# Three more chunks of 512 tokens with seven products, and two batch transforms packed closer

## The chip, the core and the metric

The kernel runs as one program on one core of a Trainium2 chip. TensorE (PE) multiplies matrices: a weight load (PEld) puts up to 128x128 numbers into the array and a matmul streams columns past them into PSUM. VectorE (DVE), ScalarE (ACT) and GpSimd (POOL) work on vectors, and the queues of SyncE (SP), ACT and POOL issue DMAs. Each engine takes its instructions in the written order. The metric is the device time of one execution in microseconds (us); lower is better.

## The reference

A real Fourier transform over the 3008 tokens of each of four batches, a complex 256x256 mixing with bias and soft threshold, the inverse transform, and then a feed-forward layer with a leaky rectifier over all 12032 tokens:

```python
X = np.fft.rfft(x, axis=1)                       # x: (4, 3008, 256)
Yr = Xr @ w_r - Xi @ w_i + b_r
Yi = Xr @ w_i + Xi @ w_r + b_i
Yr = np.sign(Yr) * np.maximum(np.abs(Yr) - 0.01, 0.0)   # Yi likewise
y = np.fft.irfft(Y, n=3008, axis=1)
h = y @ w_in                                     # (12032, 256) x (256, 2048)
g = np.maximum(h, 0.0) + alpha * np.minimum(h, 0.0)
out = g @ w_out                                  # (2048, 256)
```

## The kernel before

**Numbers in two parts.** Most operands are split into a high and a low part (`hi` by ACT, `lo = x - hi` by DVE or POOL), and a product is three matmuls: hi by hi, hi by the weights' low part, lo by hi.

**The transform of a batch** has four parts, for each of which the program has short functions. *Row parts* (`a_load`, `a_split`, `a_mm`, `a_evac`; 16 groups g per batch) go through DRAM (`ad`); *column parts* (`b_load`, `b_mm`, `b_evac`, the mixing `m_*`, `c_mm`, `c_evac`; 12 pairs q per batch) read `ad` and write `zd`. The last part (`d_load`, `d_mm`, `d_part`) reads 376 tokens of `zd`, transforms them by 16 small matmuls (L611) and splits them into `yh`, `yl`, the input of the feed-forward layer. All use the three PSUM buffers `ps_f`.

**The feed-forward layer in two forms.** The first `CC` = 24 chunks (mostly 384 tokens) go through 16 steps each: `l1_step` does six matmuls of 384 columns (L672), ACT and DVE make `q` (L678, L679) and split it (L683, L684), and `l2_step`, three steps later, does nine matmuls of 256 columns (L709 to L711). From token 8960 on six chunks of 512 tokens follow, each as eight pairs of steps (`s_l1`, `s_l2`). A pair has twelve matmuls of 512 columns (L775); then, instead of eight products of 256 columns (24 matmuls, the pairs named in `PLAIN`, and all of the last chunk), six pairs of the eight use Strassen's scheme: sums of blocks (L790 to L810) and seven products (21 matmuls, L871 to L873). It needs sums of blocks of the weights, made once by `w_full`, `w_sums`, `w_split` near the end of the main steps, in the space of the transform's tables. After a chunk's eighth pair `s_out` (L890) joins the products in PSUM by three copies on ACT and eight additions on DVE; only then are the two `ps_o` buffers free for the next chunk's products. `s_turn` transposes and stores. Chunks and their matmuls run two pairs (`SLAG`) apart.

**What sets the order.** The main steps are numbered 0 to NS - 1 (NS = 384). A table `todo` says behind which step another piece of work is written; `mid` does so for the middle of a step, `pre` and `post` for the pairs. In the main steps the batches' transforms stand at fixed distances: row groups every 2 steps, column pairs every 6, batch 2 from step 137 (rows) and 172 (columns), batch 3 from 241 and 276. The column parts of batch 2 and the row parts of batch 3 share only a few steps (239 to 246), and step 256 begins a chunk of 256 tokens. At the very start `keep_warm(WARM)` puts 40 small matmuls (L964) on PE between the row parts and the first column product of batch 0 (`b_mm`, L426).

```python
WARM = 40
o = s0 + 44 - (SHIFT if b == 2 else 0); i = o + 6 * q     # column pair q of batch b + 1
```

Of the kernel before, what the change touches and what calls it, by code (L numbers as in the profile page):

```python
# [93 lines left out]
def fft_mix_moe(ctx, tc, x, w_r, w_i, b_r, b_i, w_in, w_out, alpha, la, rb, lc, rd, lf, cf, sel, out):  # L94
# [12 lines left out]
    TC = 384  # L107
    assert NC * TC - 128 == NC * TOK

    CC = 24  # L110
    SC = 512

    def head(c):
# [9 lines left out]

    const = ctx.enter_context(tc.tile_pool(name="const", bufs=1))
    work = ctx.enter_context(tc.tile_pool(name="work", bufs=2))
    dram = ctx.enter_context(tc.tile_pool(name="dram", bufs=2, space=bass.MemoryType.DRAM))
    ps_f = ctx.enter_context(tc.tile_pool(name="ps_f", bufs=3, space=bass.MemoryType.PSUM))
    ps_h = ctx.enter_context(tc.tile_pool(name="ps_h", bufs=2, space=bass.MemoryType.PSUM))
    ps_o = ctx.enter_context(tc.tile_pool(name="ps_o", bufs=2, space=bass.MemoryType.PSUM))
# [503 lines left out]
        ds[dg] = [d_mm(t, ct) for ct in range(CT)]  # L633

    def s_dpart(dg, n):
        for k, n0, n1, a, z in s_parts(dg):
            if k == n:
                for ct in range(CT):
                    if n == NS2 - 1:
                        d_part(ds[dg][ct], ct, n0, n1, *(y[:, :, a:z] for y in yt[CC + n]))  # L640
                    else:
                        s_dput(ds[dg][ct][:, :, n0:n1], [y[:, ct] for y in yt[CC + n]], a // CH, z // CH)

    def s_dput(ps, ys, u, u1):

        ys = [y.rearrange("p (g i j) -> p g i j", i=CH, j=32) for y in ys]
        n = 0
        while u < u1:
            if u % 32 == 0 and u1 - u >= 32:
                w = (u1 - u) // 32 * 32  # L650
                src = ps[:, :, n:n + w].rearrange("p i (g j) -> p g i j", j=32)
                dst = [y[:, u // 32:(u + w) // 32] for y in ys]
            else:
                w = min(u1, u // 32 * 32 + 32) - u
                src = ps[:, :, n:n + w]
                dst = [y[:, u // 32, :, u % 32:u % 32 + w] for y in ys]
            split(src, *dst, A, V)
            u += w
            n += w

# [73 lines left out]
        for k in range(4):  # L734
            sw[k] = a[:, k], (a[:, 4 + k] if k < 2 else b[:, k - 2])

    wf = []

    def w_full(p):

        h, m = divmod(4 * p, FH)
        w = wo_h[h][:, m:m + 4]
        t = work.tile([128, 4, C], F32, tag="xt", name="wo_f")
        V.tensor_tensor(out=t, in0=f(w[:, :, 0]), in1=f(w[:, :, 1]), op=ALU.add)
        s = work.tile([128, 4, 2, 128], F32, tag="xt", name="wo_s")
        wf.extend((t.rearrange("p (r j) (c h) -> p j h r c", j=2, h=2), s))

    def w_sums(p, k):

        t, s = wf  # L750
        x, y, op = ((t[:, 0, 1], t[:, 1, 1], ALU.add), (s[:, 0], t[:, 0, 0], ALU.subtract),
                    (t[:, 0, 0], t[:, 0, 1], ALU.subtract), (t[:, 1, 0], s[:, 1], ALU.subtract))[k]
        V.tensor_tensor(out=s[:, k], in0=x, in1=y, op=op)

    def w_split(p):
        _, s = wf
        wf.clear()
        a, b = (t[:, :, 2 * p:2 * p + 2] for t in sw["all"])
        A.activation(out=a[:, 0:4], in_=s, func=AF.Copy)
        V.tensor_tensor(out=a[:, 4:6], in0=s[:, 0:2], in1=f(a[:, 0:2]), op=ALU.subtract)  # L760
        V.tensor_tensor(out=b, in0=s[:, 2:4], in1=f(a[:, 2:4]), op=ALU.subtract)


    sg, sa = {}, {}
# [125 lines left out]
    def s_out(n):  # L890
        a, b, c = sa.pop(n)
        e = [work.tile([128, HS], F32, tag="q", name="se", bufs=3) for _ in range(3)]
        u = [work.tile([128, HS], F32, tag="gh", name="su", bufs=4) for _ in range(3)]
        c1 = work.tile([128, 2, HS], F32, tag="Yt", name="c1", bufs=1)
        c2 = work.tile([128, 2, HS], F32, tag="Yc", name="c2", bufs=1)
        A.activation(out=e[0], in_=a[:, 0], func=AF.Copy)
        A.activation(out=e[1], in_=c[:, 1], func=AF.Copy)
        A.activation(out=e[2], in_=o_last[:, 1], func=AF.Copy)
        V.tensor_tensor(out=c1[:, 1], in0=a[:, 1], in1=e[0], op=ALU.add)
        V.tensor_tensor(out=u[0], in0=c[:, 0], in1=e[0], op=ALU.add)  # L900
        V.tensor_tensor(out=u[1], in0=e[2], in1=e[1], op=ALU.subtract)
# [64 lines left out]
    with tc.manual_schedule():  # L966
# [111 lines left out]
        for b in range(B):  # L1078
            s0 = b * per
            for g in range(J if b == 0 else 0, min(NCH, CC - NCH * b)):  # L1080
                i = s0 + g * FT
                at(i - 8, d_load, b, g)
                at(i - 4 if i == J * FT else i - FT + 1, d_open, NCH * b + g)
                if b == 0 and g == J:
                    at(i - DS, d_step, b, g)
                else:
                    at(i - 3, d_step, b, g)
            if b + 1 < B:
                o = s0 + 4 - (SHIFT if b == 2 else 0)
                for g in range(NG):  # L1090
                    if b == 0 and g >= FILL:
                        i = 6 * (g - FILL) + 9
                        if g % 2 == 0:
                            at(i - 8, a_load, 1, g // 2)
                        at(i, a_mm, 1, g)
                        at(i, a_evac, 1, g)
                    if b == 0:
                        continue
                    if g % 2 == 0:
                        at(o + 2 * g - 2, a_load, b + 1, g // 2)  # L1100
                    at(o + 2 * g + 3, a_split, b + 1, g)
                    at(o + 2 * g + 5, a_mm, b + 1, g)
                    at(o + 2 * g + 5, a_evac, b + 1, g)
                o = s0 + 44 - (SHIFT if b == 2 else 0)
                for q in range(NPAIR):
                    i = o + 6 * q
                    if b == 0:
                        i = PB + 11 * q // 2
                    at(i - BL, b_load, b + 1, q)
                    at(i, b_mm, b + 1, q)  # L1110
                    at(i, b_evac, b + 1, q)
                    at(i, b_evac2, b + 1, q)
                    at(i + MM, m_mm, b + 1, q)
                    at(i + M2, m_mm2, b + 1, q, when=mid)
                    for n, k in enumerate(MP):
                        at(i + k, m_part, b + 1, q, n, when=mid)
                    at(i + MP[6], m_evac1, b + 1, q)
                    at(i + CM, c_mm, b + 1, q)
                    at(i + CM, c_evac, b + 1, q)

        spairs = [(n, t) for n in range(NS2) for t in range(PR)]
        pre, post = {}, {}
        i = NS - SHIFT - 4
        at(i, w_open)
        for p in range(PR // 2):
            at(i + 5 * p, w_full, p)
            for k in range(4):
                at(i + 5 * p + 1 + k // 2, w_sums, p, k)
            at(i + 5 * p + 3, w_split, p)
        at(NS - 14, d_open, CC)  # L1130
        for dg in range(CC, B * NCH):
            ns = [n for n, *_ in s_parts(dg)]
# [43 lines left out]
        for k in range(len(spairs) + SLAG):  # L1176
# [9 lines left out]
            if k >= SLAG:  # L1186
# [42 lines left out]
```

## Time and profile before

| what | value |
|---|---|
| median of 3 runs | 1397.45 us (1396.28 to 1398.24) |
| the profiled execution | 1399.11 us, of which the span of instructions is 1397.3 us |
| PE busy | 1375.3 us, 98% |
| DVE, ACT, POOL busy | 873.9 us (63%), 728.1 us (52%), 401.0 us (29%) |
| chain that ended last | PE 86%, DVE 6%, ACT 3%, issue 2%, DMA 1% |

How to read it: matmuls overlap, so a matmul's duration (0.28 us for 256 columns) is longer than the distance from its start to the next one's start (about 0.12 us); distances of starts give PE's pace. An idle time in a row is the pause of the engine ahead of it, with what ended it. Main steps run until 1118 us, the chunks of 512 from there to the end.

### The profile page before, as it was taken

How to read it: one execution, taken by the hardware profiler on the slowest of the kernel's cores; microseconds unless marked ns; L12 is line 12 of the kernel's file. 1: busy time of each engine (PE TensorE's matmuls, PEld its weight loads, DVE VectorE, ACT ScalarE, POOL GpSimd, SP SyncE). 2: the span in 40 equal slices, each digit the busy share in tenths (PEclk: the TensorE clock that was granted, in tenths of full speed). 3: DMA queues.
4: the chain of work that ended last, by engine and by line, in shares of the span. 5: the costliest groups of instructions: out<-in, count | busy, mean ns of one | idle time of the engine just before them, and what ended most of it. 6: DMA issues, size and time to landing. Idle time of an engine off the chain costs nothing.

```text
span 1397.3 us, 25329 instructions
## 1 busy us (share of the span) xinstructions
PE 1375.3 (98%) x9670; PEld 1316.4 (94%) x9670; DVE 873.9 (63%) x1589; ACT 728.1 (52%) x1518; POOL 401.0 (29%) x454
## 2 busy tenths in 40 slices
PE   8999999999999999999999999999999999999998
PEld 4979899999999999999999999999999998898997
DVE  2666855666564544666665556666656577778874
ACT  3466555545455665454456654445454555555553
POOL 3854832322322222222222223232222211111121
PEclk9999999999999999999999999999999999999999
DMA  9864222101111231111122321111100110111001
GB/s 235 226 191 148 78 91 71 53 25 61 62 47 37 79 85 56 61 53 37 41 76 86 110 65 35 43 61 54 46 20 20 34 35 6 34 27 28 5 12 31
DMA packets 72451, 89.67 MB, mean 64 GB/s; under 512 B 22043, under 2 KB 54782, under 8 KB 72329
## 3 DMA queue, kind: packets, MB, share of 16 engines
q1 hardware_dynamic: 63743, 76.74, 18.8%
q0 software_dynamic: 5168, 8.02, 2.1%
q10 hardware_dynamic: 3418, 3.29, 0.7%
q8 instruction: 76, 1.25, 0.4%
q14 instruction: 46, 0.38, 0.1%
HBM read 50.49 MB, written 34.34 MB: 61 GB/s over the span
## 4 chain that ended last, share of the span: by engine, by line
PE 86%; DVE 6%; ACT 3%; issue 2%; DMA 1%; SPq 0%; ACTq 0%; POOL 0%; DVEq 0%
PE ps_h L672 25%; PE ps_h L775 8%; PE ps_o L710 6%; PE ps_o L711 6%; PE ps_o L709 6%; PE ps_m L486 6%; PE ps_d L611 3%; PE ps_b L426 3%; PE o_last L711 3%; PE o_last L709 3%; PE o_last L710 3%; PE ps_m L473 3%; PE ps_o L871 1%; PE ps_o L872 1%; PE ps_o L873 1%
## 5 line engine op out<-in xcount | busy, mean ns | idle before, releaser
L672 PE MATMUL ps_h<-yh,w 128*128 128x384 f32 (+1 forms) x1472 | 431.2, 335 | 3.7 <-DVE q L679 3.6
L679 DVE SCALAR_TENSOR_TENSOR q<-q,beta_s,ps_h 128x384 f32<-128x384 f32 (+1 forms) x384 | 230.7, 601 | 229.8 <-ACT q L678 227.8
L684 POOL TENSOR_TENSOR gl<-q,gh 128x384 fp32r<-128x384 f32 (+1 forms) x187 | 193.8, 1036 | 597.0 <-ACT gh L683 534.5
L683 ACT ACTIVATE gh<-q 128x384 fp32r<-128x384 f32 (+1 forms) x384 | 198.3, 516 | 274.4 <-DVE q L679 271.0
L672 PEld LDWEIGHTS ps_h<-yh,w 128*128 128x128 f32 x1472 | 271.0, 189 | 7.3 <-DVE q L679 3.8
L678 ACT ACTIVATE q<-ps_h 128x384 f32<-128x384 f32 (+1 forms) x384 | 182.7, 476 | 118.0 <-PE ps_h L672 103.4
L672 PE MATMUL ps_h<-yl,w 128*128 128x384 f32 (+1 forms) x736 | 243.4, 331 | 0.0
L711 PE MATMUL ps_o<-w,gl 128*128 128x256 f32 x768 | 216.1, 281 | 3.0 <-POOL gl L684 3.0
L710 PE MATMUL ps_o<-w,gh 128*128 128x256 f32 x768 | 216.8, 282 | 0.0
L709 PE MATMUL ps_o<-w,gh 128*128 128x256 f32 x768 | 216.0, 281 | 0.0
L684 DVE TENSOR_TENSOR gl<-q,gh 128x384 fp32r<-128x384 f32 (+1 forms) x197 | 115.9, 589 | 66.4 <-ACT gh L683 64.6
L711 PEld LDWEIGHTS ps_o<-w,gl 128*128 128x128 f32 x768 | 145.9, 190 | 3.8 <-POOL gl L684 3.6
L710 PEld LDWEIGHTS ps_o<-w,gh 128*128 128x128 f32 x768 | 145.9, 190 | 0.1
L709 PEld LDWEIGHTS ps_o<-w,gh 128*128 128x128 f32 x768 | 144.6, 188 | 0.1
L672 PEld LDWEIGHTS ps_h<-yl,w 128*128 128x128 f32 x736 | 139.3, 189 | 1.4
L775 PE MATMUL ps_h<-yh,w 128*128 128x512 f32 x384 | 128.0, 394 | 1.9 <-DVE sq L779 1.7
L711 PE MATMUL o_last<-w,gl 128*128 128x256 f32 x352 | 100.6, 286 | 0.0
L709 PE MATMUL o_last<-w,gh 128*128 128x256 f32 x352 | 100.2, 285 | 0.0
L710 PE MATMUL o_last<-w,gh 128*128 128x256 f32 x352 | 100.2, 285 | 0.0
L810 POOL TENSOR_TENSOR l<-t,h 128x512 fp32r<-128x512 f32 x30 | 38.9, 1296 | 191.2 <-ACT h L808 173.8
L775 PEld LDWEIGHTS ps_h<-yh,w 128*128 128x128 f32 x384 | 72.1, 188 | 16.8 <-DVE sq L779 2.5
L779 DVE SCALAR_TENSOR_TENSOR sq<-sq,beta_s,ps_h 128x512 f32<-128x512 f32 x96 | 68.2, 742 | 22.0 <-ACT sq L778 21.8
(209 smaller groups left out, 2727.7 us busy)
## 6 DMA issues: line engine op xcount, KB each, us to landing
zt<-zd SPq DMA_DIRECT2D x32, 384.0 KB
ad<-ast SPq DMA_DIRECT2D x48, 192.0 KB
bt<-ad SPq DMA_DIRECT2D x72, 128.0 KB
zd<-zst SPq DMA_DIRECT2D x36, 256.0 KB
xt<-in_x SPq DMA_DIRECT2D x21, 320.0 KB
cw_s<-in_moe_w_in SPq DMA_DIRECT2D x8, 512.0 KB
cw_s<-in_moe_w_out SPq DMA_DIRECT2D x8, 512.0 KB
out<-os SPq DMA_DIRECT2D x26, 128.0 KB
```

The costliest lines, as they stand in the source:

```text
L426: PE.matmul(ps[:, s, ct], t[:, s, 128 * ct:128 * ct + 128], rb_s[:, 2 * q + s], start=True, stop=True)
L486: PE.matmul(p, a[:, k:k + 128], mix[i][:, w, ct], start=(n == 0), stop=(n == 3 * CT - 1))
L672: PE.matmul(ps, wi_h[m // FH][:, w, ct, 128 * (m % FH):128 * (m % FH) + 128], a[:, ct, 0:n], start=(k == 0), stop=(k == 3 * CT - 1))
L678: A.activation(out=q, in_=ps, func=AF.Relu, scale=-1.0)
L679: V.scalar_tensor_tensor(out=q, in0=q, scalar=beta_s[:, m:m + 1], in1=ps, op0=ALU.mult, op1=ALU.add)
L683: A.activation(out=hi, in_=q, func=AF.Copy)
L684: (V if LOS[(2 * m + c) % len(LOS)] and fill or not fill and (m + c) % 2 else G).tensor_tensor(out=lo, in0=q, in1=f(hi), op=ALU.subtract)
L709: PE.matmul(a, hi[:, t], w[:, 0], start=(i, k) in first, stop=False)
L710: PE.matmul(a, hi[:, t], w[:, 1], start=False, stop=False)
L711: PE.matmul(a, lo[:, t], w[:, 0], start=False, stop=(i, k) in last)
L775: PE.matmul(ps, wi_h[m // FH][:, w, ct, 128 * (m % FH):128 * (m % FH) + 128], a[:, ct], start=(k == 0), stop=(k == 3 * CT - 1))
L779: V.scalar_tensor_tensor(out=q[:, j], in0=q[:, j], scalar=beta_s[:, m:m + 1], in1=ps, op0=ALU.mult, op1=ALU.add)
```

## The change

`CC` is 20, so chunks of 512 tokens begin at token 7424: nine instead of six, eight of them with seven products; NS is 320. In the main steps the transforms of batches 2 and 3 stand by new tables (`AO`, `BO`, `BP`): row groups every 1.5 steps from step 120 and 186, column pairs every 5 steps from 154 and 222. The sums of weights come in six instead of five steps per group, and the split of a group is four instructions in three steps. In the chunks of 512 the splits of the last transform's results are written with all high parts ahead of all low parts; a part that lies wholly in one chunk comes at pair 6 instead of 3 of its place; and a pair's sums of blocks (`s_sums`) are written behind the join of the chunk before (`s_out`) instead of ahead of it. `WARM` is 70.

```diff
-    CC = 24
+    CC = 20
-    dram = ctx.enter_context(tc.tile_pool(name="dram", bufs=2, space=bass.MemoryType.DRAM))
+    dram = ctx.enter_context(tc.tile_pool(name="dram", bufs=4, space=bass.MemoryType.DRAM))
     def s_dpart(dg, n):
...
+                        parts.extend(s_dput(ps, ys, a // CH, z // CH))
+        for src, hi, lo in parts:
+            A.activation(out=hi, in_=src, func=AF.Copy)
+        for src, hi, lo in parts:
+            V.tensor_tensor(out=lo, in0=src, in1=f(hi), op=ALU.subtract)
-    def w_split(p):
+    def w_split(p, k, low):
...
+        if not low:
+            A.activation(out=hi, in_=s[:, 2 * k:2 * k + 2], func=AF.Copy)
+        else:
+            V.tensor_tensor(out=b if k else a[:, 4:6], in0=s[:, 2 * k:2 * k + 2], in1=f(hi), op=ALU.subtract)
+        sq[n, t] = q
+
+    def s_sums(n, t):
+        q = sq.pop((n, t))
-        u = [work.tile([128, HS], F32, tag="gh", name="su", bufs=4) for _ in range(3)]
+        u = [work.tile([128, HS], F32, tag="gh", name="su", bufs=4) for _ in range(4)]
-    SHIFT = 24
+    AO = {2: 120, 3: 186}
+    BO = {2: 154, 3: 222}
+    BP = 5
-    WARM = 40
+    WARM = 70
+                    i = AO[b + 1] + 3 * g // 2
+                i = PB + 11 * q // 2 if b == 0 else BO[b + 1] + BP * q
-        i = NS - SHIFT - 4
+        i = NS - 26
-            at(i + 5 * p + 3, w_split, p)
+            for k in range(2):
+                at(i + 6 * p + 3 + k, w_split, p, k, False)
+                at(i + 6 * p + 4 + k, w_split, p, k, True)
             elif dg > CC:
-                first += 3
+                first += 6
                     if t == PR - 1:
                         s_out(n)
-                if t == 1 and n:
-                    s_turn(n - 1)
+            if k < len(spairs):
+                s_sums(*spairs[k])
+            if k >= SLAG and t == 1 and n:
+                s_turn(n - 1)
```

The first place is DVE at the join of the first chunk of 512. Before (`c` and `su` are the results of `s_out`, `dl` and `l` the low parts of a pair's blocks):

```order
L779 SCALAR_TENSOR_TENSOR sq<-sq,beta_s,ps_h 128x512 x2
L794 TENSOR_TENSOR dl<-sq,dh 128x768
L795 TENSOR_TENSOR l_13993<-sq,h_13992 128x256
L899 TENSOR_TENSOR c_14025<-ps_o,se 128x256
L900 TENSOR_TENSOR su<-ps_o,se 128x256
L901 TENSOR_TENSOR su<-se 128x256
L902 TENSOR_TENSOR su<-su,se 128x256
L903 TENSOR_TENSOR su<-ps_o,su 128x256
L904 TENSOR_TENSOR c_14025<-ps_o,su 128x256
```

And DVE at the same join in the changed kernel:

```order
L788 SCALAR_TENSOR_TENSOR sq<-sq,beta_s,ps_h 128x512 x2
L912 TENSOR_TENSOR c_12440<-ps_o,se 128x256
L913 TENSOR_TENSOR su<-ps_o,se 128x256
L914 TENSOR_TENSOR su<-se 128x256
L915 TENSOR_TENSOR su<-su,se 128x256
L916 TENSOR_TENSOR su<-ps_o,su 128x256
L917 TENSOR_TENSOR c_12440<-ps_o,su 128x256
L918 TENSOR_TENSOR c_12441<-o_last,su 128x256
L919 TENSOR_TENSOR c_12441<-su 128x256
L807 TENSOR_TENSOR dl<-sq,dh 128x768
```

The eight additions of the join now stand directly behind the pair's `sq`, and the low parts `dl`, `l` come after them.

The second place is DVE at the second group of weight sums before (`wo_s` are the sums, `sw_a` and `sw_b` their high and low parts, L679 a step's `q`):

```order
L753 TENSOR_TENSOR wo_s<-wo_f 128x256
L753 TENSOR_TENSOR wo_s<-wo_f,wo_s 128x256
L679 SCALAR_TENSOR_TENSOR q<-q,beta_s,ps_h 128x384
L760 TENSOR_TENSOR sw_a<-wo_s,sw_a 128x2x256
L761 TENSOR_TENSOR sw_b<-wo_s,sw_a 128x2x256
L679 SCALAR_TENSOR_TENSOR q<-q,beta_s,ps_h 128x384
```

And DVE at the second group in the changed kernel:

```order
L761 TENSOR_TENSOR wo_s<-wo_f 128x256
L761 TENSOR_TENSOR wo_s<-wo_f,wo_s 128x256
L687 SCALAR_TENSOR_TENSOR q<-q,beta_s,ps_h 128x384
L692 TENSOR_TENSOR gl<-q,gh 128x384
L687 SCALAR_TENSOR_TENSOR q<-q,beta_s,ps_h 128x384
L692 TENSOR_TENSOR gl<-q,gh 128x384
L770 TENSOR_TENSOR sw_a<-wo_s,sw_a 128x2x256
L687 SCALAR_TENSOR_TENSOR q<-q,beta_s,ps_h 128x384
L770 TENSOR_TENSOR sw_b<-wo_s,sw_a 128x2x256
```

The two low parts of the split no longer stand together behind one copy; each has a step's `q` ahead of it.

The third place is ACT in the changed kernel where row parts of batch 3 (`xh`, `ast`) meet column parts of batch 2 (`Yh`, `Xh`, `sm`), which lay in the same steps only from 239 to 246 before:

```order
L404 ACTIVATE ast<-ps_a 96x512
L139 ACTIVATE xh<-xt 94x512
L686 ACTIVATE q<-ps_h 128x384
L691 ACTIVATE gh<-q 128x384
L723 ACTIVATE ot<-o_last 128x256
L514 ACTIVATE Yh<-Yt 128x512
L440 ACTIVATE Xh<-ps_b 128x2x4x64
L455 ACTIVATE sm<-ps_b 128x2x2x64
L139 ACTIVATE xh<-xt 94x512
L686 ACTIVATE q<-ps_h 128x384
L691 ACTIVATE gh<-q 128x384
```

Between one step's `gh` and the next step's `q` ACT now has five other instructions here, of both transforms and of an output.

## Rows read from the trace of the kernel before

**Rows 1.** Stretches: length; busy PE, PEld, DVE, ACT, POOL; granted clock, DMA share, GB/s.

```profile
460.00:545.00 85.00, 85.00 (x578) 82.20 (x577) 40.87 (x72) 52.51 (x108) 18.58 (x21) 1.00 0.30 86
...
900.00:1000.00 100.00, 100.00 (x747) 100.00 (x746) 62.94 (x121) 49.30 (x106) 25.23 (x32) 1.00 0.15 49
...
1158.00:1298.00 140.00, 136.43 (x874) 123.10 (x873) 112.59 (x211) 74.97 (x149) 23.31 (x18) 1.00 0.10 23
```

**Rows 2.** PE in time, main steps: start, duration.

```profile
1048.35 0.34 PE L672 MATMUL ps_h<-yh,w 128*128 128x384 f32 x1
...
1050.47 0.34 PE L672 MATMUL ps_h<-yh,w 128*128 128x384 f32 x1
```

**Rows 3.** PE in time, pairs of the first chunk of 512.

```profile
1134.42 0.39 PE L775 MATMUL ps_h<-yh,w 128*128 128x512 f32 x1
...
1140.05 0.39 PE L775 MATMUL ps_h<-yh,w 128*128 128x512 f32 x1
...
1145.27 0.40 PE L775 MATMUL ps_h<-yh,w 128*128 128x512 f32 x1
...
1150.50 1.92 PE L611 MATMUL ps_d<-rd_s,zt 96*128 96x94 f32 x16
1152.20 0.48 PE L775 MATMUL ps_h<-yh,w 128*128 128x512 f32 x1
```

**Rows 4.** All engines in time, joins of the first two chunks of 512.

```profile
1169.41 0.96 DVE L794 TENSOR_TENSOR dl<-sq,dh 128x768 fp32r<-128x768 f32 x1 [0.97 <-ACT dh L790]
...
1172.41 0.41 DVE L904 TENSOR_TENSOR c<-ps_o,su 128x256 f32<-128x256 f32 x1
...
1171.80 0.28 PE L873 MATMUL ps_o<-dl,w 128*128 128x256 f32 x1
1172.88 0.38 PE L871 MATMUL ps_o<-dh,sw_a 128*128 128x256 f32 x1 [0.80 <-DVE c L904]
...
1218.51 0.25 DVE L142 TENSOR_TENSOR yl<-ps_d,yh 128x96 fp32r<-128x96 f32 x1
...
1222.71 0.50 PE L775 MATMUL ps_h<-yh,w 128*128 128x512 f32 x1 [1.57 <-DVE sq L779]
```

**Rows 5.** PE's waits from 1034 to 1118 us: total us, times, longest.

```profile
PE ps_h L672 <- DVE q L679: 2.4, 3, 1.6
```

**Rows 6.** ACT and DVE in time, second split of weight sums.

```profile
1081.22 1.05 ACT L759 ACTIVATE sw_a<-wo_s 128x1024 fp32r<-128x1024 f32 x1
...
1082.30 0.69 DVE L760 TENSOR_TENSOR sw_a<-wo_s,sw_a 128x512 fp32r<-128x512 f32 x1 [1.54 <-ACT sw_a L759]
```

**Rows 7.** PE in time, the start.

```profile
23.16 1.10 PE L387 MATMUL ps_a<-xt,lf_s 94*96 94x512 f32 x2 [1.01 <-ACT ast L404]
24.10 2.40 PE L964 MATMUL ps_idle<-idle 128*128 128x128 bf16 x40
29.30 2.05 PE L426 MATMUL ps_b<-rb_s,bt 128*128 128x128 f32 x8 [2.81 <-issue]
```

**Rows 8.** Stretches of the start, as in rows 1.

```profile
24.00:27.00 3.00, 2.50 (x41) 2.22 (x39) 0.00 (x0) 0.67 (x2) 2.89 (x4) 1.00 1.10 263
27.00:30.00 3.00, 0.69 (x3) 0.72 (x4) 0.00 (x0) 0.00 (x0) 0.37 (x1) 0.76 1.01 228
30.00:36.00 6.00, 6.00 (x26) 5.34 (x25) 2.28 (x4) 1.75 (x3) 4.29 (x8) 0.50 0.85 173
36.00:39.00 3.00, 3.00 (x16) 3.00 (x16) 0.00 (x0) 0.00 (x0) 0.59 (x2) 0.54 1.00 282
40.00:90.00 50.00, 50.00 (x357) 45.57 (x358) 42.39 (x57) 29.59 (x51) 42.43 (x51) 1.00 0.82 228
```

**Rows 9.** Tiles xt and ast, 430 to 545 us: durations ns, least, median, most.

```profile
L139 ACT ACTIVATE xh<-xt x16: 617/619/625, 453.1 to 530.9; 94x512 fp32r<-94x512 f32 x16
L142 DVE TENSOR_TENSOR xl<-xt,xh x16: 686/687/699, 453.7 to 531.6; 94x512 fp32r<-94x512 f32 x16
...
L404 ACT ACTIVATE ast<-ps_a x16: 576/594/595, 457.4 to 535.4; 96x512 f32<-96x512 f32 x16
```

More of the change, by code (lines that the diff above doesn't have):

```diff
@@ L635, in s_dpart @@
     def s_dpart(dg, n):
+        parts = []
         for k, n0, n1, a, z in s_parts(dg):
@@ L638, in s_dpart @@
                 for ct in range(CT):
+                    ps = ds[dg][ct][:, :, n0:n1]
+                    ys = [y[:, ct] for y in yt[CC + n]]
                     if n == NS2 - 1:
-                        d_part(ds[dg][ct], ct, n0, n1, *(y[:, :, a:z] for y in yt[CC + n]))
-                    else:
-                        s_dput(ds[dg][ct][:, :, n0:n1], [y[:, ct] for y in yt[CC + n]], a // CH, z // CH)
+                        hi, lo = (y[:, a:z].rearrange("p (n i) -> p n i", i=CH) for y in ys)
+                        parts.append((ps.rearrange("p i n -> p n i"), hi, lo))
+                    else:
+                        parts.extend(s_dput(ps, ys, a // CH, z // CH))
[3 more added lines that the diff above has]
+            V.tensor_tensor(out=lo, in0=src, in1=f(hi), op=ALU.subtract)
     def s_dput(ps, ys, u, u1):
@@ L656, in s_dput @@
                 dst = [y[:, u // 32, :, u % 32:u % 32 + w] for y in ys]
-            split(src, *dst, A, V)
+            yield src, *dst
             u += w
@@ L735, in w_open @@
             sw[k] = a[:, k], (a[:, 4 + k] if k < 2 else b[:, k - 2])
-    wf = []
+    wf = {}
     def w_full(p):
@@ L745, in w_full @@
         s = work.tile([128, 4, 2, 128], F32, tag="xt", name="wo_s")
-        wf.extend((t.rearrange("p (r j) (c h) -> p j h r c", j=2, h=2), s))
+        wf[p] = (t.rearrange("p (r j) (c h) -> p j h r c", j=2, h=2), s)
     def w_sums(p, k):
-        t, s = wf
+        t, s = wf[p]
         x, y, op = ((t[:, 0, 1], t[:, 1, 1], ALU.add), (s[:, 0], t[:, 0, 0], ALU.subtract),
@@ L753, in w_sums @@
         V.tensor_tensor(out=s[:, k], in0=x, in1=y, op=op)
-    def w_split(p):
-        _, s = wf
-        wf.clear()
+    def w_split(p, k, low):
+        _, s = wf[p]
         a, b = (t[:, :, 2 * p:2 * p + 2] for t in sw["all"])
[L759 to L764, printed above, removed]
+        hi = a[:, 2 * k:2 * k + 2]
+        if not low:
+            A.activation(out=hi, in_=s[:, 2 * k:2 * k + 2], func=AF.Copy)
+        else:
+            V.tensor_tensor(out=b if k else a[:, 4:6], in0=s[:, 2 * k:2 * k + 2], in1=f(hi), op=ALU.subtract)
+    sg, sa, sq = {}, {}, {}
     def s_l1(n, t):
@@ L902, in s_out @@
         V.tensor_tensor(out=u[2], in0=u[0], in1=e[1], op=ALU.subtract)
-        V.tensor_tensor(out=u[0], in0=b[:, 1], in1=u[0], op=ALU.add)
+        V.tensor_tensor(out=u[3], in0=b[:, 1], in1=u[0], op=ALU.add)
         V.tensor_tensor(out=c1[:, 0], in0=b[:, 0], in1=u[2], op=ALU.add)
-        V.tensor_tensor(out=c2[:, 1], in0=o_last[:, 0], in1=u[0], op=ALU.add)
-        V.tensor_tensor(out=c2[:, 0], in0=u[0], in1=u[1], op=ALU.add)
+        V.tensor_tensor(out=c2[:, 1], in0=o_last[:, 0], in1=u[3], op=ALU.add)
+        V.tensor_tensor(out=c2[:, 0], in0=u[3], in1=u[1], op=ALU.add)
         so[n] = c1, c2
@@ L1087, in fft_mix_moe @@
                     at(i - 3, d_step, b, g)
[L1088 to L1098, printed above, removed]
-                    if g % 2 == 0:
[L1100 to L1119, printed above, removed]
@@ new lines, in fft_mix_moe @@
+            if b == 0:
+                for g in range(FILL, NG):
+                    i = 6 * (g - FILL) + 9
+                    if g % 2 == 0:
+                        at(i - 8, a_load, 1, g // 2)
+                    at(i, a_mm, 1, g)
+                    at(i, a_evac, 1, g)
+            else:
+                for g in range(NG if b + 1 < B else 0):
+                    i = AO[b + 1] + 3 * g // 2
+                    if g % 2 == 0:
+                        at(i - 5, a_load, b + 1, g // 2)
+                    at(i - 2, a_split, b + 1, g)
+                    at(i, a_mm, b + 1, g)
+                    at(i, a_evac, b + 1, g)
@@ new lines, in fft_mix_moe @@
+            for q in range(NPAIR if b + 1 < B else 0):
+                i = PB + 11 * q // 2 if b == 0 else BO[b + 1] + BP * q
+                at(i - BL, b_load, b + 1, q)
+                at(i, b_mm, b + 1, q)
+                at(i, b_evac, b + 1, q)
+                at(i, b_evac2, b + 1, q)
+                at(i + MM, m_mm, b + 1, q)
+                at(i + M2, m_mm2, b + 1, q, when=mid)
+                for n, k in enumerate(MP):
+                    at(i + k, m_part, b + 1, q, n, when=mid)
+                at(i + MP[6], m_evac1, b + 1, q)
+                at(i + CM, c_mm, b + 1, q)
+                at(i + CM, c_evac, b + 1, q)
@@ L1121, in fft_mix_moe @@
+        done = 0
         spairs = [(n, t) for n in range(NS2) for t in range(PR)]
         pre, post = {}, {}
-        i = NS - SHIFT - 4
+        i = NS - 26
         at(i, w_open)
         for p in range(PR // 2):
-            at(i + 5 * p, w_full, p)
+            at(i + 6 * p, w_full, p)
             for k in range(4):
-                at(i + 5 * p + 1 + k // 2, w_sums, p, k)
-            at(i + 5 * p + 3, w_split, p)
+                at(i + 6 * p + 1 + k // 2, w_sums, p, k)
+            for k in range(2):
+                at(i + 6 * p + 3 + k, w_split, p, k, False)
+                at(i + 6 * p + 4 + k, w_split, p, k, True)
```

## The prediction

> **What bounds the kernel now.** I read the page first, then PE's stretches, then PE in order of time at the places that change, and last its waits. PE is busy for 98% of the span, and from 160 us on hardly anything holds it: in stretches with row groups or column pairs of a transform beside the main steps its idle time is nil [rows 1]. So time is PE's work plus a few pauses, and a change is worth the matmuls it saves plus the pauses it removes, less those it makes. The pauses are at four places. PE waits 2.81 us for batch 0's first column product, and the granted clock drops after it [rows 7, 8]. Between 1034 and 1118 us, where the weight sums are made, it waits three times for DVE [rows 5]. From 1158 to 1298 us, three joins of 512-token chunks, it is idle for 140 - 136.43 = 3.57 us [rows 1]. The fourth, in the first 160 us, is not touched.
>
> **Fewer matmuls.** Chunks 20 to 23 leave the main steps, all of 384 tokens: 4 x 16 = 64 steps. An undisturbed step takes 1050.47 - 1048.35 = 2.12 us [rows 2], so 135.7 us go. Three chunks of 512 with seven products come. A plain pair takes 1140.05 - 1134.42 = 5.63 us, a pair with seven products 5.22 [rows 3]; a chunk is 2 x 5.63 + 6 x 5.22 = 42.6 us, three are 127.7. The last transform (1.70 us of PE per 376 tokens, 1150.50 to 1152.20 [rows 3]) is the same 32 parts. Saved: 7.9 us. It is PE's own pace, so nothing else has to be faster for it.
> Of pace, the Trainium skill says something else (TensorE: Matmul & The Clock Gate, section "Wait — 56ns, not 53.3ns?"): at the full clock matmuls start one column per 2.4 GHz cycle plus about 2.5 ns apart. By it a main step would be 1.96 us, the pairs 5.21 and 4.88, and this term an estimated 6.1 us. The trace does not agree (2.12, 5.63 and 5.22 [rows 2, 3]), and the measured paces are used.
>
> **Joins.** At the first join DVE does two low parts, from 1169.41 on and after 0.97 us of waiting for ACT, before the eight additions; the sixth addition, which frees `ps_o`, starts at 1172.41, and PE, ready 0.12 after 1171.80, starts at 1172.88 [rows 4]: about 0.96 us there, and 0.5 more around it. With the additions first they come earlier by at least the first low part's 0.96 us, and by more where the wait and the second part count: the sixth ends at 1172.82 - 0.96 = 1171.9 or sooner, when PE wants it. The second join has another cause: the last transform's splits stand on DVE directly behind the additions (1218.51), and PE loses 1.57 us waiting for `sq` [rows 4]. They now come three pairs later, away from any join. What is late next: the low parts come some 2.7 us later (eight additions); queued behind them are the next pair's `sq`, for which PE has two PSUM buffers, while the products that read the parts come two pairs (over 10 us) later. DVE is busy 112.59 of 140 us [rows 1], so it can catch up, but not at once. Before, pauses of 3.57 us plus some 0.3 us at each of three joins that the modelled ends of matmuls hide, 4.5; after, I leave 0.1 at each of eight joins: 3.7 us saved. Bounds: 4.5 saved; or eight joins at 1.5 each, 12 - 4.5 = 7.5 lost. I take the first end nearly, because the rows name the two causes and both are moved.
>
> **Weight sums.** PE's three waits sum to 2.4 us [rows 5], about 3.3 with 0.3 hidden at each. ACT copies 1024 numbers in 1.05 us, DVE waits 1.54 us for that and then has two low parts in a row, with the step's `q` behind them [rows 6]. Now copies are of 512 (0.62 us in rows 9), so ACT pays 2 x 0.62 - 1.05 = 0.2 us more per group, hidden beside 2.12 us steps, and DVE has other work while it is copied. Saved 2.5; bounds 3.3 saved and 1 lost (one new meeting with a last-transform part, which now falls into the second group).
>
> **The start.** 40 filling matmuls last 2.40 us from 24.10, 0.06 us each, then PE idles until the DMA of the first column tile has landed, 29.30 [rows 7]. 70 end at about 28.3: they lie in that pause and cost nothing; if the tile came over 1.0 us sooner they would cost the difference. The pause becomes 1.0 us. The granted clock was 1.00 (2.4 GHz) before it, 0.76 on average from 27 to 30, 0.50 (1.2 GHz) to 36, 0.54 to 39, and 1.00 again from 40 [rows 8]: (0.24 x 3 + 0.5 x 6 + 0.46 x 3) / 0.5 = 10.2 us at the lower level, about 9.4 of them with work. A pause of 1.01 us just before left the clock at 1.00 [rows 7, 8]. If this one leaves it too, half of 9.4 goes, 4.7; the first pairs have latencies that a faster PE does not shorten, so 4.0. It lasts to the end of the batch because PE is busy 50.00 of 50 us there, DVE and POOL 42.4 [rows 8]. Bounds: 4.7 and nothing.
>
> **Transforms closer together.** Row groups every 1.5 steps and column pairs every 5 put the same work beside fewer steps, and in steps 186 to 217 both together, which no row shows. Alone, neither costs PE anything: 85.00 of 85 us busy with row groups (ACT 52.5), 100.00 of 100 with column pairs (DVE 62.9) [rows 1]. From below the cost is nothing; a gain is excluded, since PE waits for nothing there. From above: each of 16 row groups has 0.617 + 0.594 us of ACT and 0.687 of DVE [rows 9]; wholly uncovered, 1.9 x 16 = 30 us. ACT and DVE would still be under three quarters busy and PE has two PSUM buffers of slack, so I stay near the lower end: 2.5 us, about one wait of the longest sort in rows 5 (1.6) and a smaller one in the chunk of 256 at step 256, whose shorter steps now carry column pairs.
> The four DRAM buffers, the other weight order and the fourth `u` cost no instruction.
>
> **Sum.** -7.9 - 3.7 - 2.5 - 4.0 + 2.5 = -15.6 us. The profiled execution took 1399.11 us (span 1397.3, 1.8 around it), the median of the runs is 1397.45, 1.66 lower; the same sum from it gives 1381.9, and I say 1382.
>
> **Rivals.**
> *The clock drops all the same.* For: the pause does not vanish. Against: 1.01 us left it alone. The start's term is 0: 1386.
> *The packed transforms wait more.* Five column pairs of batch 2 meet row groups, and ACT has five instructions between two steps. For: all three `ps_f` buffers are shared. Against: rows 1. Six waits of 1.5 us instead of 2.5: 9, so 1388.5.
> *The joins do not get better* (the reorder does not do what it says): the low parts behind the additions delay `sq`, and the pause only moves, 1.5 us at eight joins. For: DVE is the busiest engine after PE there. Against: it waits 0.97 us for ACT at the join and has slack. +7.5 instead of -3.7: 1393.
> *Slower.* In steps 186 to 217 ACT waits for DVE's results of the column pair with the row group's copies and the next step's `q` queued behind it, so that PE stops in every step. Without this term the sum is -18.1; spread over 16 row groups it is even at 1.13 us per group, and at 1.9 us it gives 30 - 18.1 = +12.3: 1410. For: ACT's order puts both transforms between two steps. Against: each alone leaves PE without a pause.
>
> **How the numbers follow.** Forecast 0.52, clock 0.20, packed transforms 0.14, joins 0.08, slower 0.04, and 0.02 for no change by some mixture. The terms' best ends sum to 7.9 + 4.5 + 3.3 + 4.7 = 20.4: 1377; with a few us for the scatter of runs and the untouched pauses of the first 160 us, 1373. The upper end takes in the clock and the packed transforms, and just the joins: 1393. About 0.2% (2.8 us) is what a measurement can tell from no change: faster 0.92, within 0.04, slower 0.04.
>
> **What would show it.** Right: 24 more pairs of 5.2 and 5.6 us; after 39 us no stretch at 0.50; no wait of PE for the join's additions; less than 1 us of waits for `q` at the weight sums; PE full while both transforms run. Wrong: a clock of 0.50 after 28 us, PE waits for `ps_a` or `q` between steps 186 and 270, or waits for `sq` after each join.

## The result, and the profile after

| | before | changed |
|---|---|---|
| median of 4 runs each | 1397.85 us (1396.28 to 1399.38) | 1381.26 us (1380.92 to 1382.38) |
| profiled execution, its span | 1399.11 us, 1397.3 us | 1381.03 us, 1379.1 us |
| PE, DVE, ACT, POOL busy | 1375.3, 873.9, 728.1, 401.0 us | 1363.7, 927.3, 735.7, 398.2 us |
| chain that ended last | PE 86%, DVE 6% | PE 92%, DVE 3% |

The ratio is 0.9883 (0.9866 to 0.9900): 1.2% faster, 0.7 us under the forecast. First PE's waits over the whole execution of the changed kernel (total us, times, longest):

```profile
PE ps_o L719 <- POOL gl L692: 3.3, 3, 2.6
PE ps_c L548 <- DVE Y L500: 1.2, 1, 1.2
PE ps_h L680 <- DVE q L687: 1.2, 1, 1.2
PE ps_a L387 <- ACT ast L404: 1.1, 1, 1.1
PE ps_idle L979 <- DVE idle L985: 1.0, 1, 1.0
PE ps_d L611 <- ACT ast L404: 0.8, 1, 0.8
PE ps_b L426 <- issue: 0.6, 1, 0.6
PE ps_a L390 <- DVE hl L142: 0.5, 1, 0.5
...
```

No wait for `sq` or for a join's `c` is left, and those for `q` at the weight sums [rows 5] are gone: the one of 1.2 is in the first 160 us, which the change doesn't touch. Two are new, on `ast` (L611) and `hl`, both at the packed transforms. The stretches of the changed kernel, columns as in [rows 1, 8]:

```profile
27.00:30.00 3.00, 2.39 (x37) 2.24 (x35) 0.00 (x0) 0.00 (x0) 0.70 (x1) 1.00 1.04 248
30.00:36.00 6.00, 6.00 (x46) 5.38 (x44) 2.24 (x4) 1.65 (x3) 4.86 (x9) 1.00 0.95 192
36.00:39.00 3.00, 3.00 (x23) 2.75 (x24) 1.69 (x3) 1.73 (x3) 2.12 (x4) 1.00 1.04 334
...
585.00:680.00 95.00, 93.70 (x668) 90.35 (x667) 66.01 (x122) 55.57 (x118) 24.11 (x26) 1.00 0.38 112
1000.00:1300.00 300.00, 300.00 (x1947) 273.93 (x1947) 246.80 (x471) 168.93 (x333) 51.84 (x40) 1.00 0.09 22
```

At the start the clock stays at 1.00, where [rows 8] had 0.50. Through 300 us with at least six joins PE is never idle, against 3.57 us in 140 [rows 1]. Between 175 and 1300 us only 585 to 680 us, where row groups meet column pairs, is clearly short of full: 1.30 us idle.

One join, DVE in order of time in the changed kernel (start, duration):

```profile
1018.24 1.41 DVE L788 SCALAR_TENSOR_TENSOR sq<-sq,beta_s,ps_h 128x512 f32<-128x512 f32 x2 [0.67 <-ACT sq L787]
1019.56 0.42 DVE L912 TENSOR_TENSOR c<-ps_o,se 128x256 f32<-128x256 f32 x1
...
1021.66 0.41 DVE L917 TENSOR_TENSOR c<-ps_o,su 128x256 f32<-128x256 f32 x1
...
1022.66 0.95 DVE L807 TENSOR_TENSOR dl<-sq,dh 128x768 fp32r<-128x768 f32 x1
```

and PE's starts of four pairs in a row there:

```profile
1020.03 0.40 PE L784 MATMUL ps_h<-yh,w 128*128 128x512 f32 x1
...
1025.26 0.40 PE L784 MATMUL ps_h<-yh,w 128*128 128x512 f32 x1
...
1030.88 0.39 PE L784 MATMUL ps_h<-yh,w 128*128 128x512 f32 x1
...
1036.50 0.39 PE L784 MATMUL ps_h<-yh,w 128*128 128x512 f32 x1
```

The sixth addition (L917) ends at 1021.66 + 0.41 = 1022.07, before PE has finished the pair's twelve matmuls (L784) that began at 1020.03; `dl` no longer waits for ACT, as it did for 0.97 us [rows 4]. The pairs stand 5.23, 5.62 and 5.62 us apart, the paces of [rows 3], across a join.

To sort the difference I split each profiled execution at the first matmul of the main steps. Before:

```profile
111.38 0.36 PE L672 MATMUL ps_h<-yh,w 128*128 128x256 f32 x1
```

Changed:

```profile
107.37 0.36 PE L680 MATMUL ps_h<-yh,w 128*128 128x256 f32 x1
```

In this pair of executions the start gave 4.0 us, and the rest (span less this) went from 1285.9 to 1271.7 us, 14.2 less. Within the rest the chunks of 512 can be told apart as well, by the first and the last start of a first-layer matmul. Before (six chunks, 269.05 us):

```profile
1114.34 0.39 PE L775 MATMUL ps_h<-yh,w 128*128 128x512 f32 x1
...
1383.39 0.39 PE L775 MATMUL ps_h<-yh,w 128*128 128x512 f32 x1
```

Changed (nine chunks, 398.3 us):

```profile
966.80 0.39 PE L784 MATMUL ps_h<-yh,w 128*128 128x512 f32 x1
...
1365.11 0.39 PE L784 MATMUL ps_h<-yh,w 128*128 128x512 f32 x1
```

The experiments use these numbers: medians for what a kernel gains, the others for where.

### The profile page after: what moved, and what is told of

It reads as the page before. It is cut to its first block, busy times and chain, and to the rows that moved or that the text cites. A ratio compares the mean times of both kernels' runs of the same rounds, so it can differ in the third digit from the quotient of the medians.

```text
span 1379.1 us, 25262 instructions
## 1 busy us (share of the span) xinstructions
PE 1363.7 (99%) x9550; PEld 1295.2 (94%) x9550; DVE 927.3 (67%) x1689; ACT 735.7 (53%) x1519; POOL 398.2 (29%) x432
## 4 chain that ended last, share of the span: by engine, by line
PE 92%; DVE 3%; DMA 1%; ACT 1%; issue 1%; POOL 0%; SPq 0%; ACTq 0%; DVEq 0%; POOLq 0%
PE ps_h L680 22%; PE ps_h L784 14%; PE ps_m L486 5%; PE ps_o L718 5%; PE ps_o L719 5%; PE ps_o L717 5%; PE ps_d L611 4%; PE ps_o L885 3%; PE ps_b L426 3%; PE ps_o L886 3%; PE ps_o L884 3%; PE ps_m L473 3%; PE o_last L719 2%; PE o_last L717 2%; PE o_last L718 2%
## 5 line engine op out<-in xcount | busy, mean ns | idle before, releaser
L680 PE MATMUL ps_h<-yh,w 128*128 128x384 f32 (+1 forms) x1216 | 354.1, 334 | 1.3 <-DVE q L687 1.2
L687 DVE SCALAR_TENSOR_TENSOR q<-q,beta_s,ps_h 128x384 f32<-128x384 f32 (+1 forms) x320 | 191.6, 599 | 165.7 <-ACT q L686 162.9
L680 PE MATMUL ps_h<-yl,w 128*128 128x384 f32 (+1 forms) x608 | 200.4, 330 | 0.0
L784 PE MATMUL ps_h<-yh,w 128*128 128x512 f32 x576 | 191.3, 393 | 0.0
L719 PE MATMUL ps_o<-w,gl 128*128 128x256 f32 x640 | 180.4, 282 | 3.3 <-POOL gl L692 3.3
L718 PE MATMUL ps_o<-w,gh 128*128 128x256 f32 x640 | 180.6, 282 | 0.0
L717 PE MATMUL ps_o<-w,gh 128*128 128x256 f32 x640 | 180.0, 281 | 0.0
L784 PEld LDWEIGHTS ps_h<-yh,w 128*128 128x128 f32 x576 | 108.2, 188 | 21.3
L718 PEld LDWEIGHTS ps_o<-w,gh 128*128 128x128 f32 x640 | 121.5, 190 | 0.1
L717 PEld LDWEIGHTS ps_o<-w,gh 128*128 128x128 f32 x640 | 120.6, 188 | 0.1
L784 PE MATMUL ps_h<-yl,w 128*128 128x512 f32 x288 | 112.9, 392 | 0.0
L787 ACT ACTIVATE sq<-ps_h 128x512 f32<-128x512 f32 x144 | 82.3, 593 | 34.1 <-PE ps_h L784 33.4
L803 ACT ACTIVATE dh<-sq 128x768 fp32r<-128x768 f32 x64 | 54.1, 846 | 72.1 <-DVE sq L788 37.9
```

What stands on the lines that cost most here:

```text
L687: V.scalar_tensor_tensor(out=q, in0=q, scalar=beta_s[:, m:m + 1], in1=ps, op0=ALU.mult, op1=ALU.add)
L717: PE.matmul(a, hi[:, t], w[:, 0], start=(i, k) in first, stop=False)
L718: PE.matmul(a, hi[:, t], w[:, 1], start=False, stop=False)
L719: PE.matmul(a, lo[:, t], w[:, 0], start=False, stop=(i, k) in last)
```

## The experiments

Each was timed in 5 rounds, which gave 4 to 6 executions (11 of before, filling 70). "Start" is the first main step's matmul, "rest" the span less it, "512" the time from the first to the last start of a first-layer matmul in the chunks of 512, all of the one profiled execution. The first, second, fourth and eighth kernel of the table ran on one chip; before with filling 70, both, parts at pair 3 and rows apart on a second; the other four on a third. Medians are compared on one chip where that is possible.

| kernel | median, us (lowest to highest) | ratio to before | start | rest | 512 |
|---|---|---|---|---|---|
| changed, again | 1384.00 (1381.27 to 1387.04) | 0.9907 (0.9892 to 0.9923) | 109.44 | 1275.7 | 398.3 |
| filling 40 | 1383.72 (1381.42 to 1387.06) | 0.9909 (0.9892 to 0.9925) | 109.09 | 1271.4 | 398.3 |
| before, filling 70 | 1396.63 (1395.35 to 1397.50) | 0.9992 (0.9984 to 1.0001) | 108.79 | 1286.1 | 269.0 (six) |
| sums first | 1384.91 (1384.28 to 1386.53) | 0.9919 (0.9906 to 0.9933) | 108.92 | 1274.0 | 400.9 |
| splits alternating | 1385.21 (1384.22 to 1387.32) | 0.9909 (0.9893 to 0.9924) | 109.60 | 1275.7 | 400.1 |
| both | 1392.07 (1390.63 to 1392.35) | 0.9957 (0.9942 to 0.9972) | 107.91 | 1282.2 | 408.0 |
| parts at pair 3 | 1381.16 (1380.11 to 1381.81) | 0.9882 (0.9867 to 0.9897) | 107.46 | 1271.4 | 398.4 |
| chunks from 8960 | 1390.92 (1388.47 to 1391.69) | 0.9956 (0.9943 to 0.9969) | 108.69 | 1281.2 | 263.3 (six) |
| weights as before | 1386.39 (1385.63 to 1387.18) | 0.9915 (0.9900 to 0.9930) | 109.17 | 1274.8 | 398.3 |
| rows apart | 1380.27 (1378.84 to 1381.65) | 0.9876 (0.9860 to 0.9892) | 110.39 | 1269.3 | 398.3 |
| rows apart, one `gl` on DVE | 1380.25 (1380.02 to 1383.38) | 0.9878 (0.9859 to 0.9898) | 108.24 | 1270.0 | 398.3 |
| one `gl` on DVE | 1384.13 (1381.44 to 1385.14) | 0.9895 (0.9878 to 0.9912) | 108.81 | 1271.9 | 398.3 |

Where an edit doesn't touch the chunks of 512 their time is the same to 0.1 us, so a change of it there is the edit's. The start isn't as steady: with 70 filling matmuls it lies between 107.46 and 110.39 us in these kernels, and the 107.37 of the changed kernel's first execution is earlier than all of them.

**The changed kernel again.**

> The changed kernel once more, on the chip of the next three, as their base. Every theory expects 1381.3 us, within 1.5, and a ratio to the kernel before of 0.988.

No edit. The runs spread over 5.8 us. The profiled one is the slowest, its rest 4.0 us longer than the first time's. The place is the meeting of the transforms. ACT, then PE, first in the earlier execution:

```profile
655.45 0.59 ACT L404 ACTIVATE ast<-ps_a 96x512 f32<-96x512 f32 x1 [0.52 <-DMA ad<-ast]
...
664.54 0.58 ACT L404 ACTIVATE ast<-ps_a 96x512 f32<-96x512 f32 x1
...
665.17 1.13 PE L611 MATMUL ps_d<-rd_s,zt 96*128 96x94 f32 x8 [0.83 <-ACT ast L404]
```

and in this one, with a stretch behind it:

```profile
658.81 0.59 ACT L404 ACTIVATE ast<-ps_a 96x512 f32<-96x512 f32 x1 [2.06 <-DMA ad<-ast]
...
667.90 0.58 ACT L404 ACTIVATE ast<-ps_a 96x512 f32<-96x512 f32 x1
...
668.54 2.02 PE L611 MATMUL ps_d<-rd_s,zt 96*128 96x94 f32 x8 [2.37 <-ACT ast L404]
```

```profile
668.00:675.00 7.00, 6.46 (x26) 6.06 (x27) 4.94 (x10) 3.99 (x11) 1.14 (x2) 0.53 0.31 94
```

ACT waits for the store of an earlier `ast` to DRAM before it writes `ast` again, 0.52 us in one execution and 2.06 in the other. Later PE waits for another `ast`, the copy that empties a shared `ps_f` buffer for L611 (0.83, 2.37), and in the second execution the granted clock then falls to its lower level. That copy starts 9.09 us behind the one that waited, in both executions, so ACT's 1.54 us more reach PE whole; in all nine kept traces in which ACT waits for the store here, PE's wait is ACT's and 0.3 us. That the meeting of the transforms makes the place, the next experiment shows.

**Row groups away from column pairs.**

```diff
-    AO = {2: 120, 3: 186}
-    BO = {2: 154, 3: 222}
+    AO = {2: 120, 3: 144}
+    BO = {2: 168, 3: 230}
```

> The changed kernel with the row groups of batch 3 at steps 144 to 166, and the column pairs of batch 2 from 168 and of batch 3 from 230, so that row groups and column pairs never share a step. Theory after the last runs: the two pauses at steps 189 and 205 (0.8 us, and 1.1 to 5.4 us with a fall of the clock) come from ACT waiting for the store of a row group's result (zst has two buffers) with both transforms' work behind it; both go: -1.8 us against the best execution, -3 to -5 against the median of the last call (1384.0), and less scatter. Rival, the density of column pairs makes them: no change, pauses stay.

Batch 3's row groups now come directly behind batch 2's, before the column pairs. The same stretch as above, with all of it full, and the clock at 1.00:

```profile
585.00:680.00 95.00, 95.00 (x715) 95.00 (x714) 63.07 (x121) 48.05 (x102) 27.72 (x33) 1.00 0.17 54
```

The rest is 2.4 us shorter than that of the changed kernel. So the meeting costs 2.4 us in a good execution, more in one like the above. PE has no wait for `ast` or `hl` left behind the first 160 us: row groups every 1.5 steps cost nothing where no column pairs lie beside them.

**One low part of the early steps from POOL to DVE**, alone and with rows apart: `(V if (c, m) == (0, 7) or ...` in the choice of `gl`'s engine.

> The kernel with row groups and column pairs apart, and one low part (L692, chunk 0, step 7) made by DVE instead of POOL, where it stood behind three weight conversions and PE paused 2.9 us at 155 us, with the clock at 0.50 for 3.4 us after it. Theory: pause and fall go, -3 to -4.6 us against rows apart (1380.3), so 1376 to 1377.5. Rival, DVE is as full there and the pause moves to its next instruction: -1 to +1.

> The changed kernel with that one low part on DVE and nothing else. Theory: -3 to -4.6 us against the changed kernel, and 1 to 2 us slower than with rows apart. Rival: no change.

Neither gains. PE's waits from 140 to 175 us in the changed kernel:

```profile
PE ps_o L719 <- POOL gl L692: 2.9, 2, 2.6
```

and with one `gl` on DVE:

```profile
PE ps_o L719 <- POOL gl L692: 2.3, 1, 2.3
PE ps_h L680 <- DVE q L687: 1.8, 2, 1.2
```

The wait is shared out between the two engines, and with 4.1 us it is not shorter than the 2.9; the rest is 1271.9 us against 1271.7, although the clock stayed at 1.00 there. Between the kernels with this edit, on one chip, rows apart is worth 3.9 us of the medians and 1.9 of the rest.

**The filling matmuls**, in the changed kernel and in the kernel before:

```diff
-    WARM = 70
+    WARM = 40
```

> The changed kernel with 40 filling matmuls again instead of 70. My theory: the pause of some 2.8 us comes back ahead of the first column product, the granted clock stands at 0.50 from 28 to 39 us, the first main step starts at about 111.4 us instead of 107.4, and all after it is as much later: +4.0 us (3.5 to 4.5). Rival, the start has slack: the later work (conversion of weights on DVE and POOL) sets the pace and takes the loss up: +0 to +1.

```diff
-    WARM = 40
+    WARM = 70
```

> The kernel before with 70 filling matmuls and nothing else. My prediction's term: -4.0 us. Rival formed on the last call, where 40 matmuls cost nothing measurable and the clock fell for 3.4 us only in that execution: the column tiles' DMAs set the start of the pairs, the length of the fall differs between executions, and the median gains 0 to 1.5 us. Both expect no stretch at 0.50 before 100 us.

Neither moves the median by more than 0.5 us; in the changed kernel five executions each, spread over nearly 6 us, could hide a difference of 2 or 3. With 40, PE and the stretches of the start (changed kernel):

```profile
29.72 2.69 PE L426 MATMUL ps_b<-rb_s,bt 128*128 128x128 f32 x11 [2.74 <-issue]
```

```profile
27.00:30.00 3.00, 0.28 (x1) 0.31 (x2) 0.00 (x0) 0.00 (x0) 0.81 (x1) 0.93 1.03 203
30.00:36.00 6.00, 6.00 (x36) 5.63 (x36) 2.45 (x4) 1.76 (x3) 3.90 (x7) 0.75 0.83 189
36.00:39.00 3.00, 3.00 (x24) 2.63 (x23) 0.00 (x0) 1.24 (x3) 2.00 (x5) 1.00 0.97 237
```

The pause is that of [rows 7] (2.74 against 2.81), but the lower level lasted (0.07 x 3 + 0.25 x 6) / 0.5 = 3.4 us, not 10.2; that costs 1.7 us at most, and the first main step comes at 109.09 us, against 109.44 with 70 in the changed kernel again. The kernel before, filled with 70, keeps the clock up,

```profile
30.00:36.00 6.00, 5.34 (x39) 4.85 (x40) 2.24 (x4) 1.65 (x3) 3.88 (x7) 1.00 0.88 205
36.00:39.00 3.00, 3.00 (x24) 2.63 (x23) 0.27 (x1) 1.54 (x3) 2.31 (x5) 1.00 1.06 265
```

and its interval still holds no change. The other executions have no trace, but each has its mean granted clock on record. Of 35 executions of the kernel before, timed beside these experiments, 13 have 0.996 or less (mean time 1399.3 us) and 19 have 0.998 or more (1396.2); with 70 none of 11 is under 0.998. So it seems that the long fall comes in some of before's executions only, that it costs about 3 us there, and that the filling removes it; that the fall of the untraced ones lies at the start is not shown. The median hardly sees it.

**Sums ahead of the join.**

```diff
                 s_l1(*spairs[k])
+                s_sums(*spairs[k])
             do(post, k)
...
-            if k < len(spairs):
-                s_sums(*spairs[k])
```

> The changed kernel with the sums of blocks written ahead of the join again (all else as changed: splits packed, parts three pairs later). My theory: low parts stand ahead of the join's additions on DVE, PE waits for the additions as before, some 1.4 us at each of eight joins: +11 us (8 to 12). Rival, the packed and moved splits alone removed the pauses, and the order of sums is worth nothing: +0 to +1.

The old order comes back: `dl` waits for ACT, the sixth addition starts 2.9 us after it, PE waits for it. DVE at the join near 1113 us:

```profile
1113.16 0.96 DVE L807 TENSOR_TENSOR dl<-sq,dh 128x768 fp32r<-128x768 f32 x1 [0.97 <-ACT dh L803]
...
1116.05 0.41 DVE L917 TENSOR_TENSOR c<-ps_o,su 128x256 f32<-128x256 f32 x1
```

PE there:

```profile
1116.51 0.38 PE L884 MATMUL ps_o<-dh,sw_a 128*128 128x256 f32 x1 [0.39 <-DVE c L917]
```

But it waits 0.39 us and not 0.80 [rows 4], and the chunks of 512 take only 2.6 us more: over eight joins this edit by itself is worth far less than 1.4 us per join. Both the theory and its rival missed.

**Splits alternating**, each high part followed by its low part, with the new order of the sums, and then with the old:

```diff
-            A.activation(out=hi, in_=src, func=AF.Copy)
-        for src, hi, lo in parts:
-            V.tensor_tensor(out=lo, in0=src, in1=f(hi), op=ALU.subtract)
+            split(src, hi, lo, A, V)
```

> The changed kernel with high and low parts of the last transform's splits alternating again; sums of blocks stay behind the join, whole parts three pairs later. Sums first alone cost about 3 us, both edits together about 11. Theory, the order of the join decides and late splits only add where the join comes behind the sums: +0 to +2. Rival, the splits' length is the main cause: +7 to +8, the two costs add up.

> The changed kernel with the sums of blocks ahead of the join and high and low parts alternating again (whole parts stay three pairs later). Theory after the last call, where sums first made pauses of 0.35 to 0.55 us at four joins only: DVE comes to the join later when the splits alternate, by some 0.8 us, and both together give the 1.4 us per join of before: +9 to +12 against the changed kernel, +7 to +9 against sums first. Rival, the two edits do not add up: the same as sums first, +3.

Alternating alone, DVE at a place with a last transform (the first two rows of six low parts):

```profile
1224.76 0.26 DVE L142 TENSOR_TENSOR yl<-ps_d,yh 128x96 fp32r<-128x96 f32 x1 [0.30 <-ACT yh L139]
1225.48 0.42 DVE L142 TENSOR_TENSOR yl<-ps_d,yh 128x256 fp32r<-128x256 f32 x1 [0.45 <-ACT yh L139]
...
```

DVE waits for ACT again and again. The rest is 4.0 us longer than the changed kernel's, but 2.2 of that lies ahead of the chunks of 512, where this execution met the long pause of the transforms (1.1 us on `ast` for 0.8, and a fall of the clock); in the chunks the edit costs 1.8 us. Both together take 9.7 us more there:

```profile
968.16 0.39 PE L782 MATMUL ps_h<-yh,w 128*128 128x512 f32 x1
...
1376.16 0.39 PE L782 MATMUL ps_h<-yh,w 128*128 128x512 f32 x1
```

PE's waits from 1000 to 1300 us, sums first:

```profile
PE ps_o L884 <- DVE c L917: 0.9, 3, 0.4
```

and with both:

```profile
PE ps_o L882 <- DVE c L915: 3.4, 6, 0.7
PE ps_h L782 <- DVE sq L786: 0.8, 4, 0.3
PE ps_o L882 <- DVE c L910: 0.5, 3, 0.2
```

The two edits compound: 2.6 and 1.8 apart, 9.7 together, so the theories of both runs held. That a DVE which is late from one cause has no slack left for the other fits these waits, but where the lateness is handed on I didn't trace.

**Last-transform parts at pair 3**, as before: `first += 3`.

> The changed kernel with the whole parts of the last transform back at pair 3 of their place (18, 42 and 58 instead of 21, 45 and 61), right behind a join. My theory: DVE has the eight additions, the low parts of a pair and six splits in a row there, and PE waits for sq as at the second join before, 1.6 us at two joins: +3.3 us (2 to 4). Rival, high parts ahead of low parts alone took the pause away: +0 to +0.5.

Nothing: the same time in the chunks of 512, and no wait of PE from 900 us on. So with packed splits and the sums behind the join the place doesn't matter; with the old orders it was not tried by itself.

**Chunks of 512 from 8960**, all else as changed: `CC = 24`.

> The changed kernel with the chunks of 512 from token 8960 on again (six instead of nine, 384 main steps), all else as changed. My theory: 64 main steps of 2.12 us come back and 24 pairs of 5.32 go: +7.9 us (7.4 to 8.5). Rival by matmul counts at one column per cycle and 2.5 ns (the Trainium skill, TensorE: Matmul & The Clock Gate): +6.1. Rival, the seven products gain nothing, since DVE is nearly the bound there, and the whole gain came from pauses: 0 to +2.

The rest is 9.5 us longer, but this execution also has the long pause and a fall of the clock at 668 us, worth about 2.3 us against the changed kernel's (0.56 us more idle from 655 to 680 us, mean clock 0.93 against 1.00 of 25 us), and from 150 to 175 us it is 0.6 us better off; some 7.7 remain. The medians, on one chip, differ by 6.9. This kernel also shows the joins by themselves: its six chunks of 512 are those of before with the new orders, and they take 263.3 us against 269.05, 5.8 less.

**Weight sums as before** (five steps a group, one copy, two low parts):

```diff
+        A.activation(out=a[:, 0:4], in_=s, func=AF.Copy)
+        V.tensor_tensor(out=a[:, 4:6], in0=s[:, 0:2], in1=f(a[:, 0:2]), op=ALU.subtract)
+        V.tensor_tensor(out=b, in0=s[:, 2:4], in1=f(a[:, 2:4]), op=ALU.subtract)
...
+            at(i + 5 * p + 3, w_split, p)
```

> The changed kernel with the weight sums as before: groups five steps apart, one copy of 1024 numbers and both low parts in one step. My theory: DVE waits for the copy with the step's q behind it, PE's pauses of before (some 4 us between the first group and the chunks of 512) come back: +4 us (2.5 to 4.5). Rival, those pauses came from meeting the last transform's splits, which now lie at other steps: +0 to +1.

DVE has [rows 6] again:

```profile
939.60 0.69 DVE L767 TENSOR_TENSOR sw_a<-wo_s,sw_a 128x512 fp32r<-128x512 f32 x1 [1.55 <-ACT sw_a L766]
```

and PE waits for `q` from 895 to 960 us, where the changed kernel doesn't wait:

```profile
PE ps_h L680 <- DVE q L687: 2.3, 3, 1.7
```

The rest is 3.1 us longer.

## Why the prediction was right, and where it wasn't

The time was right to 0.7 us in the first set of runs (2.0 in the second, with 1384.00), but its terms were off both ways and cancelled; that the number came out so close is luck.

- **Fewer matmuls (-7.9)**: right. There are 24 more pairs (L784 with `yh` counts 576 against 384 at L775), which take 5.23 and 5.62 us, and the experiment gives 7.7. The pace of the Trainium skill (TensorE: Matmul & The Clock Gate, section "Wait — 56ns, not 53.3ns?") gave an estimated 6.1; the runs side with the trace.
- **Joins (-3.7)**: the sign, the place and the first cause right, the size too small. Over six chunks the term is 5.8 us; by difference, 14.2 - 7.9 + 2.4 - 3.1 = 5.6. The mis-sized step is "pauses of 3.57 us plus some 0.3 us at each of three joins ... 4.5": by PE's starts the kernel before pauses at seven places in its chunks of 512, each some 0.27 us longer than its row says, 5.6 us in all. And of the 0.8 us that I left there is nothing. Of the causes, the move of the parts was not needed: at pair 3 they cost nothing once the splits are packed and the sums stand behind the join. It may still help in the old orders: both undone, with the parts at pair 6, no wait for `sq` is over 0.3 us, against 1.57 [rows 4]. What the two other edits are worth is shown: undone alone 2.6 and 1.8 us, both 9.7, over eight joins.
- **Weight sums (-2.5)**: mechanism right, size under: 3.1.
- **The start (-4.0)**: mis-sized for the median. The profiled pair does differ by 4.0 us there, and the clock stays up as I argued, but filling 70 gives the kernel before 0.5 us in the median and the changed one nothing that could be measured. The step that failed is the 10.2 us at the lower level, read from one execution, which was 1.7 us over the median of the first runs; with the same pause of 2.7 us another execution had 3.4. The mean clocks on record suggest that most of before's executions don't have the long fall.
- **Transforms (+2.5)**: right in size by luck of the execution: 2.4 from the meeting of both, and 4.0 more where ACT waits longer for the store of `ast`. I had named PSUM and ACT's order; the rows show that path (a copy in ACT's order empties the buffer that PE needs), but what sets it off is the store, which I had not named.

The rest is accounted for: -7.9 - 5.8 - 3.1 + 2.4 = -14.4 us against 14.2 less measured. The edits that were not undone by themselves (the four DRAM buffers, the fourth `u`, the later `s_turn`) therefore have little left to explain. With the start at -0.5 the sum is -14.9; the medians of the changed kernel lie 16.6 and 12.1 us under before's in the two sets of runs. Of the rivals, the first (the clock drops all the same) didn't happen, yet its price for the start, nothing, was nearly right. The joins' rival and the two on the transforms fell: PE is full at the joins, and the meeting makes two pauses (0.8 and 0.5 us in the first execution), not six or one in every step. Open is why some executions of the changed kernel wait longer for that store. The best version is rows apart: 3.9 us below its like with one `gl` on DVE, on one chip. Without that edit 1380.27 against 1381.26, on two chips, would not tell the two apart; its trace does, by the pause that is gone.

## What to carry to other kernels

Before pricing a clock fall, or any pause behind a DMA, look at it in more than one execution: one profile gave 4 us for what is worth 0.5 in the median. Where an engine in the written order has to serve a join, put first what frees the buffers, and write all the high parts of a split ahead of all the low ones; test such edits together as well as apart, since their costs can compound. Be wary of two transforms that share an engine and PSUM buffers in the same steps: what holds one of them is handed on along the engine's order.

## What the hardware showed that I had not expected

Around 150 to 175 us the longer pause isn't always the one followed by the lower clock. Changed kernel, then splits alternating, same columns as above:

```profile
150.00:175.00 25.00, 22.05 (x151) 21.48 (x150) 17.55 (x27) 13.57 (x29) 19.43 (x17) 0.93 0.09 27
```

```profile
150.00:175.00 25.00, 20.88 (x150) 20.34 (x148) 18.89 (x25) 14.20 (x29) 21.35 (x18) 1.00 0.16 41
```

PE idles 2.95 us in the first and the mean clock is 0.93; in the second it idles 4.12 and the clock stays at 1.00. The time to the end hardly differs for it: one `gl` on DVE has 1.00 here and a rest of 1271.9 us, parts at pair 3 has 0.93 and 1271.4. That another engine than PE sets the pace there would fit, but is not shown. And the same store of `ast` held ACT 0.52 us in one execution and 2.06 in another.
